# Half sums of g and softmax normalizations in another order on VectorE, in a fused sparse-attention and PReLU-MLP kernel

## The chip, the cores and the metric

The kernel runs on one core of one Trainium2 chip. The metric is device time in microseconds (us). One execution was also recorded by the hardware profiler; all durations of single instructions are from that execution. Engines are named as in the profile: PE is TensorE (matmuls, with PEld for its weight loads), DVE is VectorE, ACT is ScalarE, POOL is GpSimd, SP issues most of the DMAs.

## What is computed

Two things in a row. First, sparse attention for 8 batches, 8 heads, 576 tokens and a head dimension of 64: four heads look at the last 32 tokens, four at every 32nd token. Then a two-layer MLP on the 4608 token rows of width 512, with 2048 hidden values and a PReLU:

```
scores = where(mask, q @ k.T / 8, -1e9);  attn = softmax(scores);  x = attn @ v      # 4608 x 512
h = x @ w_in                                                                          # 4608 x 2048
g = max(h, 0) + alpha * min(h, 0)
out = g @ w_out                                                                       # 4608 x 512
```

## The kernel before, in words

**Chunks.** The MLP runs over nine chunks of 512 rows, n = 0 to 8. Layer 1 of a chunk is sixteen pieces (`lin1_piece`, L596): four matmuls of 128x512 into a PSUM bank (L608), ACT makes relu(-h) (L616), and DVE combines both into a 128x512 block of g in fp16 (L619). The attention of later batches is woven in between: after each piece of the MLP, `attn_n` (L827) runs none, one or two attention steps from a long list (L500 to L570).

**Layer 2 with fewer multiplications.** For chunks 2 to 8 (`FAST = 2`) layer 2 is `lin2_fast` (L696), Strassen's scheme in Winograd's form: seven products of half-size blocks in place of eight. It needs four sums of the blocks of g, `gsum[0]` to `gsum[3]`, as the stationary operand of some of its matmuls. `g_sum(n, z, h, eng)` (L666) makes half h of sum z: one `tensor_tensor` on 128x1024 fp16 values (L677), with both inputs and the output in SBUF. In the text, (z,h) stands for that half sum. (2,0) and (0,0) are made on POOL during layer 1; the other six are made on DVE.

Each of the fourteen steps of `lin2_fast` is eight matmuls of 128x256. Steps 16 and 17 of the chunk's loop need g alone. Step 18 needs half 0 of sum 0, step 19 half 1 of it: (0,1). Step 20 needs (1,0), step 21 needs (1,1). Steps 22 and 23 need g, steps 24 and 25 sum 2, steps 26 and 27 sum 3, steps 28 and 29 g.

**Attention steps.** A pair is two heads of a batch. `score_both` (L356) makes the scores of a pair: matmuls into the bank `sp` and two banks `sph` (L376), exponentials on ACT (L399 and L405), and the mask by multiplication on POOL (L401 and L408). `pv_piece` (L413) multiplies by v into a bank `pv` (L429, six or four small matmuls), then DVE takes the reciprocal of the row sums (L436) and multiplies (L438). These two DVE instructions together are called a normalization here. A pair of the strided heads has three such pieces, and the last of them is followed by the DMA transpose of the pair's result on SP (L468).

**Banks.** `pv`, `sph` and the transposes of q and k share one pool of three PSUM banks, `pspool` (L63), handed out in turn: the fourth tile waits until the first one's reader is through. For `pv` that reader is the second instruction of the normalization.

**Order.** Every engine runs its instructions in the order of the program (`keep_in_program_order`), so a half sum's place on DVE is where the loop of L953 calls `g_sum`: after the piece of the MLP and the attention steps of step i, by the table `sums` (L949). Counting L964 to L967 out gives, with P for a normalization:

| chunk | attention in steps 16 to 22 |
|---|---|
| 2 | 16: transposes of q; 17: P (pair 14, second); 19: transposes of k; 20: P (pair 14, third); 21: scores; 22: P |
| 3, 4, 5 | 16: P (first of pair 18, 22, 26); 17: P (second); 19: P (third); 20: scores; 21: P (first of the next pair) |
| 6 | 16: scores; 17: P (first of pair 30); 19: P (second); 20: P (third); 22: P |
| 7, 8 | none, the attention is over |

Of the kernel before, what the change touches and what calls it, by code (L numbers as in the profile page):

```python
# [32 lines left out]
def kernel(  # L33
# [540 lines left out]
    def attn_until(b):  # L574

        return max(i for i, (g, _) in enumerate(pieces) if g == 4 * b + 3) + 1
# [3 lines left out]
    def attn_step(end):  # L580
        while late:
            late.pop(0)()
        if pos["i"] < end:
            pieces[pos["i"]][1]()
            pos["i"] += 1
        if defer:
            defer.pop(0)()
        while after:
            after.pop(0)()
# [6 lines left out]
    def lin1_piece(n, m, begin=False):  # L596
        if n not in gTs:
            gTs[n] = gpool.tile([128, 16, 512], F16, tag="gT", name="gT")
        c0 = (512 * n) % RING
        hps = begun.pop(m, None)  # L600
        if hps is None:
            pool, tag = (pspool, "ps") if n == 0 and m // 3 % 2 else (phpool, "hps")
            hps = pool.tile([128, 512], F32, tag=tag, name="hps")
            order = (2, 3, 0, 1)
        else:
            order = (0, 1)
        for kk in order[0:2] if begin else order:
            keep(nc.tensor.matmul(  # L608
                hps, win16[:, kk, 128 * m : 128 * m + 128], xT[:, kk, c0 : c0 + 512],
                start=(kk == 2), stop=(kk == 1)))  # L610
        if begin:
            begun[m] = hps
            return

        neg = npool.tile([128, 512], F32, tag="neg", name="neg")
        keep(nc.scalar.activation(neg, hps, AF.Relu, scale=-1.0))  # L616

        def fin():
            keep(nc.vector.scalar_tensor_tensor(  # L619
                gTs[n][:, m, :], neg, oma[:, m : m + 1], hps, op0=ALU.mult, op1=ALU.add))  # L620
        late.append(fin)
# [3 lines left out]
    def lin2_piece(n, i):  # L625
        mt, part = i // 4, i % 4
        last = n == NCH - 1
        if part == 0:
            ops_cur["t"] = phpool.tile([128, 512], F32, tag="hps", name="ops")
        ops = ops_cur["t"]  # L630
        r0 = 512 * n + 128 * mt
        if last and mt == 3:

            if part in (1, 3):
                return
            c0 = 128 * part
            half = phpool.tile([128, 512], F32, tag="hps", name="ops3") if part else ops
            for kf in range(16):
                keep(nc.tensor.matmul(
                    half[:, 0:256], gTs[n][:, kf, 128 * mt : 128 * mt + 128],  # L640
                    wout16[:, kf, c0 : c0 + 256], start=(kf == 0), stop=(kf == 15)))
            osb = opool.tile([128, 512], F32, tag="osb", name="osb")
            keep(nc.vector.tensor_copy(osb[:, 0:256], half[:, 0:256]))
            keep(nc.sync.dma_start(out[r0 : r0 + 128, c0 : c0 + 256], osb[:, 0:256]))
            return
        for kf in range(4 * part, 4 * part + 4):
            keep(nc.tensor.matmul(  # L647
                ops, gTs[n][:, kf, 128 * mt : 128 * mt + 128], wout16[:, kf, :],
                start=(kf == 0), stop=(kf == 15)))
        if part == 3:  # L650
            osb = opool.tile([128, 512], F32, tag="osb", name="osb")
            keep(nc.scalar.copy(osb, ops))
            keep(nc.sync.dma_start(out[r0 : r0 + 128, :], osb))


    def wout_sum(i):

        def w(j, c):
            return wout16.rearrange("p (i j) c -> p i j c", j=2)[:, :, j, 256 * c : 256 * c + 256]

        o, a, b = (
            (0, w(0, 1), w(0, 0)), (1, w(1, 1), wsum[0]),
            (2, w(1, 1), w(0, 1)), (3, w(1, 0), wsum[1]))[i]
        keep(nc.vector.tensor_tensor(wsum[o], a, b, op=ALU.subtract))

    def g_sum(n, i, h, eng="dve"):  # L666

        gv = gTs[n].rearrange("p (i j) c -> p i j c", j=2)
        hs = slice(4 * h, 4 * h + 4)

        def g(t, j):
            return gv[:, hs, j, 256 * t : 256 * t + 256]

        a, b, op = (
            (g(1, 0), g(1, 1), ALU.add), (gsum[0][:, hs], g(0, 0), ALU.subtract),
            (g(0, 0), g(1, 0), ALU.subtract), (g(0, 1), gsum[1][:, hs], ALU.subtract))[i]
        keep((nc.vector if eng == "dve" else nc.gpsimd).tensor_tensor(gsum[i][:, hs], a, b, op=op))  # L677
# [149 lines left out]
    def attn_n(n, end):  # L827
        for _ in range(n):
            attn_step(end)
        if n == 0:  # L830
            attn_step(0)
# [109 lines left out]
    for pr in range(2):  # L941
# [5 lines left out]

    FAST = 2
    sums = {  # L949
        5: [(2, 0, "pool")], 9: [(0, 0, "pool")], 15: [(0, 1, "dve"), (1, 0, "dve")],  # L950
        16: [(1, 1, "dve")], 18: [(2, 1, "dve")], 19: [(3, 0, "dve")], 20: [(3, 1, "dve")]}

    for n in range(1, NCH):  # L953
        ab = attn_until(n + 1) if n + 1 < B else len(pieces)
        left = ab - pos["i"]
        acc = -1.5 if n == 1 else 0.0
        for i in range(32 if n < FAST else 30):
            if i < 16:
                lin1_piece(n, i if n < FAST else 8 * (i // 8) + 2 * (i % 4) + i % 8 // 4)
            elif n < FAST:  # L960
                lin2_piece(n, i - 16)
            else:
                lin2_fast(n, i - 16)
            acc += left / (22 if n < FAST else 19.5 if n == B - 2 else 21) * (0.5 if i < 16 else 1.0)  # L964
            cnt = int(acc)
            acc -= cnt
            attn_n(cnt, ab)  # L967
            if n < FAST:
                if i in (18, 21, 24, 27):
                    wout_sum((i - 18) // 3)  # L970
                continue
            for z, h, eng in sums.get(i, ()):
                g_sum(n, z, h, eng)
        while pos["i"] < ab:
            attn_step(ab)
# [30 lines left out]
```

## Time and profile before

| what | value |
|---|---|
| median of 3 runs | 299.93 us (299.72 to 301.21) |
| the profiled execution | 299.7 us |
| its span, first to last instruction of the program | 297.8 us |
| half sums on DVE | 42, of 0.68 us each where nothing holds them up |
| half sums on POOL | 14, of 2.12 us |
| normalizations' multiplications (L438) | 62, mean 0.53 us |

How to read the views: a timeline has one row for a run of like instructions on one engine, with its start (us from the span's start), its length, the engine and line, the operation, output and inputs, and how many there are (x16). In square brackets stands how long the engine was idle ahead of it and who ended that. A PE row's length includes the pipeline's drain, so the next row can start before the row's end; distances between starts are what counts.

### The profile page before, as it was taken

How to read it: one execution, taken by the hardware profiler on the slowest of the kernel's cores; microseconds unless marked ns; L12 is line 12 of the kernel's file. 1: busy time of each engine (PE TensorE's matmuls, PEld its weight loads, DVE VectorE, ACT ScalarE, POOL GpSimd, SP SyncE). 2: the span in 40 equal slices, each digit the busy share in tenths (PEclk: the TensorE clock that was granted, in tenths of full speed). 3: DMA queues.
4: the chain of work that ended last, by engine and by line, in shares of the span. 5: the costliest groups of instructions: out<-in, count | busy, mean ns of one | idle time of the engine just before them, and what ended most of it. 6: DMA issues, size and time to landing. Idle time of an engine off the chain costs nothing.

```text
span 297.8 us, 6836 instructions
## 1 busy us (share of the span) xinstructions
PE 292.2 (98%) x2684; PEld 183.0 (61%) x2684; DVE 219.3 (74%) x406; ACT 178.4 (60%) x332; POOL 175.1 (59%) x164
## 2 busy tenths in 40 slices
PE   8999999999999999999999999999999999999995
PEld 3764554544554477646864686468745964784484
DVE  5688886768776897588848984898489948926852
ACT  1777756597557774775477647764676356516730
POOL 8471580059869998979896987595563405002300
PEclk9999999999999999999999999999999999999999
DMA  7999999998995969999999999987711140022004
GB/s 189 257 197 201 263 194 265 223 213 267 126 207 121 121 94 108 212 145 132 138 156 171 152 145 161 182 106 78 212 22 21 23 142 2 0 73 70 0 2 142
DMA packets 96976, 41.18 MB, mean 138 GB/s; under 512 B 75360, under 2 KB 93232, under 8 KB 96944
## 3 DMA queue, kind: packets, MB, share of 16 engines
q0 software_dynamic: 51008, 17.77, 58.4%
q1 hardware_dynamic: 45584, 22.32, 35.1%
q10 hardware_dynamic: 352, 0.66, 0.8%
q8 instruction: 21, 0.34, 0.5%
q14 instruction: 11, 0.09, 0.1%
HBM read 38.24 MB, written 9.44 MB: 160 GB/s over the span
## 4 chain that ended last, share of the span: by engine, by line
PE 85%; DVE 7%; ACT 4%; issue 3%; DVEq 0%; ACTq 0%
PE hps L608 38%; PE ops L743 18%; PE ops L647 5%; PE ops L733 5%; PE pv L429 4%; PE ops L908 3%; PE wps L785 3%; DVE gsum L677 2%; PE sp L376 2%; DVE gT L619 2%; DVE x16s L438 2%; PE sph L376 1%; ACT neg L616 1%; PE xp L454 1%; PE ops L923 1%
## 5 line engine op out<-in xcount | busy, mean ns | idle before, releaser
L608 PE MATMUL hps<-xT,win 128*128 128x512 f16 x576 | 132.4, 379 | 0.0
L619 DVE SCALAR_TENSOR_TENSOR gT<-neg,oma,hps 128x512 f16<-128x512 f32 x144 | 105.3, 744 | 36.3 <-ACT neg L616 28.5
L616 ACT ACTIVATE neg<-hps 128x512 f32<-128x512 f32 x144 | 85.8, 598 | 34.4 <-PE hps L608 32.2
L608 PEld LDWEIGHTS <-win 128*128 128x128 f16 x576 | 53.5, 98 | 58.2 <-issue 0.2
L677 POOL TENSOR_TENSOR gsum<-gT 128x1024 f16<-128x1024 f16 x14 | 29.7, 2124 | 41.7 <-DVE gT L619 36.7
L401 POOL TENSOR_TENSOR et<-et,consts 128x576 f16<-128x576 f16 (+1 forms) x24 | 35.5, 1478 | 29.3 <-ACT et L399 29.2
L743 PEld LDWEIGHTS <-gT 128*128 128x128 f16 x336 | 31.5, 98 | 5.4 <-issue 0.3
L438 DVE TENSOR_TENSOR x<-pv,rc 96x384 f16<-96x384 f32 (+2 forms) x62 | 33.0, 532 | 2.1
L408 POOL TENSOR_TENSOR et<-et,consts 128x576 f16<-128x576 f16 (+1 forms) x24 | 31.4, 1309 | 0.0
L429 PEld LDWEIGHTS <-et 72*128 72x128 f16 (+1 forms) x448 | 23.5, 98 | 12.0 <-DVE et L396 1.1
L743 PE MATMUL ops<-wout,gT 128*128 128x256 f16 x224 | 27.9, 272 | 0.1
L733 PE MATMUL ops<-wsum,gsum 128*128 128x256 f16 x216 | 26.6, 273 | 0.0
L399 ACT ACTIVATE et<-sp 128x576 f16<-128x576 f32 (+1 forms) x24 | 15.5, 644 | 17.1 <-PE sp L376 17.1
L234 POOL COPY vs<-stv 72x1024 f16<-72x1024 f16 x14 | 15.3, 1103 | 15.7 <-DMA stv<-in_v_dram 15.7
L743 PEld LDWEIGHTS <-gsum 128*128 128x128 f16 x224 | 20.9, 98 | 2.6
L733 PEld LDWEIGHTS <-gsum 128*128 128x128 f16 x224 | 20.8, 98 | 2.6
L436 DVE RECIPROCAL rc<-pv 72x6 f32<-72x6 f32 (+2 forms) x80 | 14.7, 184 | 9.8 <-PE pv L429 9.5
L688 DVE TENSOR_TENSOR osb<-ops,par 128x512 f32<-128x512 f32 (+1 forms) x14 | 9.4, 673 | 15.7 <-PE ops L743 8.2
L405 ACT ACTIVATE et<-sph 128x288 f16<-128x288 f32 (+1 forms) x48 | 18.8, 409 | 0.0
L686 ACT COPY osb<-ops 128x512 f32<-128x512 f32 x14 | 8.2, 586 | 16.8 <-PE ops L743 16.7
L647 PE MATMUL ops<-wout,gT 128*128 128x512 f16 x64 | 16.4, 379 | 0.0
L429 PE MATMUL pv<-vs,et 72*128 72x65 f16 x256 | 15.4, 193 | 0.8 <-DVE et L396 0.6
(110 smaller groups left out, 356.5 us busy)
## 6 DMA issues: line engine op xcount, KB each, us to landing
out_dram<-osb SPq DMA_DIRECT2D x35, 256.0 KB, 4.3
vl<-in_v_dram POOLq DMA_DIRECT2D x6, 384.0 KB, 9.3
win<-in_moe_w_in_dram POOLq DMA_DIRECT2D x4, 512.0 KB, 16.6
wout<-in_moe_w_out_dram POOLq DMA_DIRECT2D x4, 512.0 KB, 15.6
qsd<-in_q_dram POOLq DMA_DIRECT2D x7, 288.0 KB, 6.7
ksd<-in_k_dram POOLq DMA_DIRECT2D x7, 288.0 KB, 7.2
stv<-in_v_dram POOLq DMA_DIRECT2D x7, 288.0 KB, 7.8
ql<-in_q_dram SPq DMA_DIRECT2D x3, 576.0 KB, 7.1
```

Source lines behind the costliest of these rows:

```text
L401: keep(nc.gpsimd.tensor_tensor(mv, mv, m, op=ALU.mult))
L405: keep(nc.scalar.activation(ev[:, n * y : n * y + n], sps[y][0:r, 0:n], AF.Exp, scale=SCALE))
L408: keep(nc.gpsimd.tensor_tensor(mv, mv, m, op=ALU.mult))
L429: keep(nc.tensor.matmul(pv[:, 65 * x : 65 * x + 65], et[0:r, c : c + 128], v16[0:r, 2 * P.pr + hh, t, :] if P.strided else v16[:, 6 * (2 * ...
L438: keep(nc.vector.tensor_tensor(P.x16[0:w, c0 : c0 + 64 * nb].rearrange("r (c e) -> r c e", e=64), pvv[:, :, 0:64], rc[0:w, 0:nb].unsqueeze ...
L608: keep(nc.tensor.matmul(hps, win16[:, kk, 128 * m : 128 * m + 128], xT[:, kk, c0 : c0 + 512], start=(kk == 2), stop=(kk == 1)))
L616: keep(nc.scalar.activation(neg, hps, AF.Relu, scale=-1.0))
L619: keep(nc.vector.scalar_tensor_tensor(gTs[n][:, m, :], neg, oma[:, m : m + 1], hps, op0=ALU.mult, op1=ALU.add))
L647: keep(nc.tensor.matmul(ops, gTs[n][:, kf, 128 * mt : 128 * mt + 128], wout16[:, kf, :], start=(kf == 0), stop=(kf == 15)))
L677: keep((nc.vector if eng == "dve" else nc.gpsimd).tensor_tensor(gsum[i][:, hs], a, b, op=op))
L733: keep(nc.tensor.matmul(o, gsum[i][:, y, 128 * z : 128 * z + 128], wsum[i][:, y, :], start=(x == "5" and y == 0 and (z == 0 or alone)), st ...
L743: keep(nc.tensor.matmul(o, lhs(y), rhs(y), start=(first and y == 0), stop=(y == 7), skip_group_check=True))
```

## The change

Two tables take the place of one: `sums2` for chunk 2, and a later `sums` for chunks 3 to 8.

```diff
     sums = {
-        5: [(2, 0, "pool")], 9: [(0, 0, "pool")], 15: [(0, 1, "dve"), (1, 0, "dve")],
-        16: [(1, 1, "dve")], 18: [(2, 1, "dve")], 19: [(3, 0, "dve")], 20: [(3, 1, "dve")]}
+        5: [(2, 0, "pool")], 9: [(0, 0, "pool")], 16: [(0, 1, "dve"), (1, 0, "dve")],
+        17: [(1, 1, "dve")], 19: [(2, 1, "dve")], 20: [(3, 0, "dve"), (3, 1, "dve")]}
+    sums2 = {
+        5: [(2, 0, "pool")], 9: [(0, 0, "pool")], 15: [(0, 1, "dve")],
+        17: [(1, 0, "dve"), (1, 1, "dve")], 19: [(2, 1, "dve")], 20: [(3, 0, "dve"), (3, 1, "dve")]}
...
-            for z, h, eng in sums.get(i, ()):
+            for z, h, eng in (sums2 if n == FAST else sums).get(i, ()):
                 g_sum(n, z, h, eng)
```

The sums themselves, their engines, and the two on POOL stay as they are. On DVE the order from step 15 to step 21 becomes, with "g" for the last block of g (L619) and P1, P2, P3 for the three normalizations of the pair in work:

| chunk | before | after |
|---|---|---|
| 2 | g, (0,1), (1,0), (1,1), P2, (2,1), (3,0), P3, (3,1) | g, (0,1), P2, (1,0), (1,1), (2,1), P3, (3,0), (3,1) |
| 3, 4, 5 | g, (0,1), (1,0), P1, (1,1), P2, (2,1), P3, (3,0), (3,1) | g, P1, (0,1), (1,0), P2, (1,1), P3, (2,1), (3,0), (3,1) |
| 6 | g, (0,1), (1,0), (1,1), P1, (2,1), P2, (3,0), P3, (3,1) | g, (0,1), (1,0), P1, (1,1), P2, (2,1), P3, (3,0), (3,1) |
| 7, 8 | g, (0,1), (1,0), (1,1), (2,1), (3,0), (3,1) | the same |

## The prediction

> **What bounds the kernel now.** I read the page's totals first, then the sums of each chunk, the list of waits, and last the timelines of PE, DVE and POOL around steps 16 to 21.
>
> ```profile
> span 297.8 us, 6836 instructions
> PE 292.2 (98%) x2684; PEld 183.0 (61%) x2684; DVE 219.3 (74%) x406; ACT 178.4 (60%) x332; POOL 175.1 (59%) x164
> ```
>
> PE is the bound: nothing else is busy for more than three quarters of the span. The sums by stage give chunk 3, from the first matmul of its layer 1 to that of chunk 4 (columns: us, then PE, PEld, DVE, ACT and POOL busy, each with its count, clock, DMA share, GB/s):
>
> ```profile
> 122.47:152.78 30.31, 30.25 (x298) 20.02 (x296) 23.34 (x44) 18.70 (x35) 27.13 (x25) 1.00 1.33 153
> ```
>
> PE is busy 30.25 of 30.31 us there, at the full clock. A PE row's length holds the drain of its pipeline, so a short pause is hidden in that figure. What the change can win is time in which PE stands still, and the list of waits names two such places that end with a normalization on DVE (columns: us in total, times, longest).
>
> ```profile
> PEld L376 <- DVE x16s L438: 0.6, 3, 0.2
> PEld L429 <- DVE x16s L438: 0.5, 1, 0.5
> ```
>
> Three waits of a score matmul and one of a `pv` matmul, each for the second instruction of a normalization. The three are in chunks 3, 4 and 5, the one in chunk 2. These numbers are idle time of the weight loader, not PE's loss, so I measure the loss on PE's own rows. Chunk 3:
>
> ```profile
> 138.51 0.35 PE L429 MATMUL pv<-vs,et 72*128 72x65 f16 x6
> 139.75 1.91 PE L733 MATMUL ops<-wsum,gsum 128*128 128x256 f16 x16
> 141.50 0.29 PE L429 MATMUL pv<-vs,et 72*128 72x65 f16 x4
> 141.62 1.04 PE L733 MATMUL ops<-wsum,gsum 128*128 128x256 f16 x8
> 142.59 0.30 PE L376 MATMUL sp<-qT,kT 64*128 64x96 f16 x6
> 142.73 0.56 PE L376 MATMUL sph<-qT,kT 64*128 64x96 f16 x6
> 143.22 1.05 PE L733 MATMUL ops<-wsum,gsum 128*128 128x256 f16 x8
> 144.22 0.34 PE L429 MATMUL pv<-vs,et 72*128 72x65 f16 x6
> ```
>
> Undisturbed, sixteen matmuls take 141.50 - 139.75 = 1.75 us from start to start, 0.109 each, so eight take 0.875. The `sph` group of 142.73 takes 0.49 until the next row. In chunk 2 the same group follows without a wait:
>
> ```profile
> 111.14 1.05 PE L733 MATMUL ops<-wsum,gsum 128*128 128x256 f16 x8
> 112.44 0.30 PE L429 MATMUL pv<-vs,et 72*128 72x65 f16 x4 [0.25 <-DVE x16s L438]
> ...
> 113.68 0.29 PE L376 MATMUL sph<-qT,kT 64*128 64x96 f16 x6
> 113.90 1.05 PE L743 MATMUL ops<-wout,gT 128*128 128x256 f16 x8
> ```
>
> There it takes 0.22. So chunk 3 loses 0.49 - 0.22 = 0.27 us at `sph`. The eight matmuls at 143.22 take 1.00 until `pv` at 144.22: 0.125 more than 0.875, a second, smaller loss. In chunk 2, the eight at 111.14 take 1.30 until `pv`: 0.43 lost. Chunk 5 shows the same two losses as chunk 3 (0.49 and 1.00):
>
> ```profile
> 203.36 0.56 PE L376 MATMUL sph<-qT,kT 64*128 64x96 f16 x6
> 203.85 1.05 PE L733 MATMUL ops<-wsum,gsum 128*128 128x256 f16 x8
> 204.85 0.34 PE L429 MATMUL pv<-vs,et 72*128 72x65 f16 x6
> ```
>
> **Why PE waits there.** The three banks of `pspool` go round. In chunk 3 the order is P1, P2, P3, `sph`, `sph`, next `pv`: the second `sph` takes P2's bank, the next `pv` takes P3's. In chunk 2 two transposes of k stand between, and P3's `pv` takes P2's bank. DVE in chunk 3:
>
> ```profile
> 137.60 1.61 DVE L619 SCALAR_TENSOR_TENSOR gT<-neg,oma,hps 128x512 f16<-128x512 f32 x2 [0.47 <-ACT neg L616]
> 139.25 1.10 DVE L677 TENSOR_TENSOR gsum<-gT 128x1024 f16<-128x1024 f16 x1
> 140.27 0.68 DVE L677 TENSOR_TENSOR gsum<-gsum,gT 128x1024 f16<-128x1024 f16 x1
> 140.87 0.18 DVE L436 RECIPROCAL rc<-pv 72x6 f32<-72x6 f32 x1
> 141.09 0.55 DVE L438 TENSOR_TENSOR x16s<-pv,rc 72x384 f16<-72x384 f32 x1
> 141.56 0.68 DVE L677 TENSOR_TENSOR gsum<-gsum,gT 128x1024 f16<-128x1024 f16 x1
> 142.38 0.55 DVE L438 TENSOR_TENSOR x16s<-pv,rc 72x384 f16<-72x384 f32 x1
> 143.66 0.42 DVE L438 TENSOR_TENSOR x16s<-pv,rc 72x256 f16<-72x256 f32 x1
> ```
>
> P2 ends at 142.38 + 0.55 = 142.93, and PE loads the weights of the `sph` matmul that waited 0.06 later:
>
> ```profile
> 142.99 0.15 PEld L376 LDWEIGHTS <-kT 64*128 64x128 f16 x5 [0.20 <-DVE x16s L438]
> ```
>
> P3 ends at 144.08, and `pv` starts at 144.22. DVE works without a pause from 139.25 on, with three half sums ahead of P2 and four ahead of P3.
>
> **The change, part by part.** Nothing is added or removed: six half sums a chunk stay, none issues a DMA, no row of POOL's or SP's program moves. Only DVE's order changes. From the rows above, a sum holds DVE for 140.87 - 140.27 = 0.60 when undisturbed, a normalization of six for 0.22 (140.87 to 141.09) plus 0.47 (141.09 to 141.56) = 0.69; a result is complete 0.08 after the next instruction starts.
>
> *Chunks 3, 4, 5, the gain.* P1 can start as soon as the last g is off, 139.21 - 0.08 = 139.13, as its `pv` (138.51 + 0.35) is done. P1 runs to 139.82, then (0,1) to 140.42, (1,0) to 141.02, P2 until 141.71 with its result at 141.79. The second `sph` is due at 142.73: it no longer waits. Then (1,1) until 142.31, and P3 with its result at 142.31 + 0.22 + 0.42 = 142.95, over 0.8 ahead of the next `pv`, which then comes at about 143.8. Both losses go: 0.27 + 0.125 = 0.395 a chunk, 1.19 in three.
>
> *Chunks 3, 4, 5, the price.* (0,1) moves behind P1, and step 19 waits for it; behind that wait stands the rest of PE's program. Its first matmul is due at 139.75 + 8 x 0.109 = 140.62. By the above, (0,1) starts at 139.82, ends at 139.82 + 0.68 = 140.50, and with 0.06 for the signal PE has it at 140.56: in time by 0.06. That holds if the sum takes 0.68. In the row it takes 1.10, and the next thing to decide is why.
>
> ```profile
> 107.57 1.27 POOL L401 TENSOR_TENSOR et<-et,consts 72x576 f16<-72x576 f16 x1
> 108.81 1.73 POOL L408 TENSOR_TENSOR et<-et,consts 72x576 f16<-72x576 f16 x1
> ...
> 138.51 1.28 POOL L408 TENSOR_TENSOR et<-et,consts 72x576 f16<-72x576 f16 x1
> 139.73 2.98 POOL L116 DMA_DIRECT2D kr<-in_k_dram x4
> ```
>
> ```profile
> 108.28 1.12 DVE L677 TENSOR_TENSOR gsum<-gT 128x1024 f16<-128x1024 f16 x1
> 109.33 2.36 DVE L677 TENSOR_TENSOR gsum<-gsum,gT 128x1024 f16<-128x1024 f16 x2
> 111.83 0.55 DVE L438 TENSOR_TENSOR x16s<-pv,rc 72x384 f16<-72x384 f32 x1
> ...
> 257.70 0.69 DVE L677 TENSOR_TENSOR gsum<-gT 128x1024 f16<-128x1024 f16 x1
> ```
>
> In chunk 3 a mask runs on POOL from 138.51 to 139.79, and the sum's 0.60 of work, counted back from 140.27, begins at 139.67, as the mask ends. In chunk 2 the first sum overlaps a mask that ends at 108.84 and finishes 0.6 after that; the second mask then stretches to 1.73 and the second sum ends about 0.6 after it. In chunk 7, with no masks left, the same first sum takes 0.69. So the long sums are sums that stood behind a mask. In the new order P1, which reads PSUM, fills the time until the mask is off: (0,1) starts at 139.82, 0.15 after 139.67. I take 0.68, the nearest row, and keep 1.10 as the other end: then (0,1) ends at 140.92, and PE waits until 140.98, 0.36 a chunk, 1.1 in three.
>
> The Trainium skill ("SBUF — State Buffer", section "SBUF: two separate sides") says that VectorE and GpSimd share one pair of SBUF ports under a lock that is held for a whole instruction, and that a VectorE operation with two SBUF inputs takes part in this against a GpSimd operation that reads SBUF. The rows above agree with it: first come, first served, and the loser stands still. By it the sum costs 0.68 in its new place; by the row taken as it stands, 1.10.
>
> *Chunk 2.* (0,1) keeps its place and ends at 109.40. P2 follows at 109.33, ends at 110.10, where it ended at 112.38. P3's `pv`, due at 111.14 + 0.875, has its bank: 0.43 gone. (1,0) moves behind P2, but it stood behind the mask until 110.5 anyway, and still ends 0.68 before the pair's end, 109.33 + 2.36 - 0.60 = 111.09, when step 20 starts as before. (1,1) ends at 111.69, due at 112.15.
>
> *Chunk 6* has scores in step 16, so the first two sums keep their place, and its `pv` banks were never late. *Chunks 7 and 8* have the same order as before. All zero. *What is late next:* (2,1) follows P3 in chunk 3 and ends at about 143.6; step 24, which reads it, lies sixteen matmuls (1.75) behind the `pv` of 143.8, at 145.7 or later. (3,0) and (3,1) end 1.2 after (2,1), and step 26 is sixteen matmuls further. The DMA transpose on SP follows P3 and starts earlier.
>
> The sum: 0.43 + 1.19 = 1.6 at most, less up to 0.05 a chunk for a sum that is just in time: **1.5 us**. Between these places PE is busy without a pause, and the other engines follow it, so what PE wins stays. Against the profiled execution: 299.7 - 1.5 = 298.2. The median lies 0.2 above that execution, so 298.4.
>
> **The rivals.**
>
> *The sum stays long (1.10) wherever it stands.* Then PE waits 0.36 in step 19 of three chunks: gain 1.5 - 1.1 = 0.4, 299.5. For it: it is the first sum behind g in all rows of 1.10. Against it: chunk 7's 0.69.
>
> *The waits were not worth their length*: PE, early by 1.5 us, waits somewhere else for ACT, DVE or a load, and the time stays at about 299.9. For it: DVE is 74% busy. Against it: no other wait of this kind stands in the list, and ACT, POOL and DVE take their pace from PE in each chunk.
>
> *Slower.* (0,1) meets a mask that starts ahead of it. It now starts 0.57 later, so a POOL operation that begins between 139.25 and 139.82 gets in front, and the sum waits for it, 1.27 as in the row of 107.57. PE would stand from 140.62 until 141.83, 1.2 a chunk, 3.6 in three, against 1.5 won: 302.0. It decides from the point where POOL's mask begins 0.7 later than in the row of 138.51. Against it: the mask of 138.51 is the last before four DMA issues at 139.73, and POOL's place is set by ACT and so by PE. The Trainium skill's rule of the lock ("SBUF — State Buffer", section "SBUF: two separate sides") would let this happen; no row shows it behind P1.
>
> *More than forecast.* All of the 1.6 comes, and the runs fall, like the lowest of those before, 0.2 below the median from which I count: 298.1 or less.
>
> **How the numbers follow.** Forecast 0.60, long sum 0.14, no gain 0.11, slower 0.06, more than forecast 0.09. A measurement of this kernel tells about 0.5% from no change, 1.50 us: faster means below 298.43. The forecast's own range, 298.0 to 298.9, straddles that, so I split it: 0.31 below, 0.29 above. Faster 0.31 + 0.09 = 0.40; same 0.29 + 0.14 + 0.11 = 0.54; slower 0.06. The range reaches from 297.9 to 300.1: it holds the forecast, the long sum and no gain, and leaves out the slower case and part of the last.
>
> **What would show it.** Right: no wait of L376 or L429 for x16s in chunks 2 to 5; the `sph` group 0.22 from start to next row; (0,1) after P1, 0.68 long, and sixteen matmuls of steps 18 and 19 in 1.75; chunk 3 at 29.9 us. Wrong: a gap in the middle of these sixteen, a sum of 1.1 behind P1, or the same 0.4 us lost elsewhere in the chunk.

## The result and the profile after

| | median | lowest to highest | runs |
|---|---|---|---|
| before | 299.87 us | 298.85 to 301.21 | 12 |
| changed | 298.35 us | 297.80 to 299.17 | 12 |

The ratio is 0.9952, with a 95% interval of 0.9937 to 0.9967: 1.45 us faster (1.0 to 1.9). The forecast was 298.4. That it lies 0.05 from the median is luck: the interval is 0.9 us wide.

The profiled execution of the changed kernel spans 296.8 us, 1.0 less than the one of before. The rest is hidden by its start: it reaches chunk 2 0.48 later, ahead of anything that the change touches. The clean measure is PE's first matmul of each chunk. First the rows before:

```profile
90.85 2.32 PE L608 MATMUL hps<-xT,win 128*128 128x512 f16 x10
...
122.31 1.89 PE L608 MATMUL hps<-xT,win 128*128 128x512 f16 x8
...
213.24 1.03 PE L608 MATMUL hps<-xT,win 128*128 128x512 f16 x4
```

The first row is chunk 2's, the second chunk 3's, the third chunk 6's. The same three in the changed kernel:

```profile
91.33 1.89 PE L608 MATMUL hps<-xT,win 128*128 128x512 f16 x8
...
122.38 0.81 PE L608 MATMUL hps<-xT,win 128*128 128x512 f16 x3
...
212.19 1.24 PE L608 MATMUL hps<-xT,win 128*128 128x512 f16 x5
```

Chunk 2 goes from 31.46 to 31.05 us, 0.41 less. Chunks 3 to 5 go from 90.93 to 89.81, 1.12 less, 0.37 each. From there to the end it is 84.6 in both. Together 1.53.

In the list of waits no weight load waits for `x16s` any more. (`x16s` is where the normalizations P1, P2 and P3 write: 18 multiplications. The 62 of the table ahead of the prediction are those that write `x`.) In chunk 2 of the changed kernel `pv` of step 20 comes 0.88 after the eight matmuls ahead of it, where it came 1.30 after:

```profile
111.64 1.05 PE L733 MATMUL ops<-wsum,gsum 128*128 128x256 f16 x8
112.52 0.29 PE L429 MATMUL pv<-vs,et 72*128 72x65 f16 x4
```

PE in chunk 3 of the changed kernel:

```profile
138.59 0.35 PE L429 MATMUL pv<-vs,et 72*128 72x65 f16 x6
...
139.83 1.91 PE L733 MATMUL ops<-wsum,gsum 128*128 128x256 f16 x16
141.58 0.29 PE L429 MATMUL pv<-vs,et 72*128 72x65 f16 x4
141.71 1.04 PE L733 MATMUL ops<-wsum,gsum 128*128 128x256 f16 x8
142.68 0.30 PE L376 MATMUL sp<-qT,kT 64*128 64x96 f16 x6
142.81 0.29 PE L376 MATMUL sph<-qT,kT 64*128 64x96 f16 x6
143.04 1.05 PE L733 MATMUL ops<-wsum,gsum 128*128 128x256 f16 x8
143.92 0.35 PE L429 MATMUL pv<-vs,et 72*128 72x65 f16 x6
```

The `sph` group takes 0.23 from its start to the next row where it took 0.49, the eight matmuls behind it 0.88 where they took 1.00, and the sixteen of steps 18 and 19 still take 1.75. DVE and POOL in the same place:

```profile
139.43 0.55 DVE L438 TENSOR_TENSOR x16s<-pv,rc 72x384 f16<-72x384 f32 x1
139.91 0.68 DVE L677 TENSOR_TENSOR gsum<-gT 128x1024 f16<-128x1024 f16 x1
140.50 0.68 DVE L677 TENSOR_TENSOR gsum<-gsum,gT 128x1024 f16<-128x1024 f16 x1
...
141.32 0.55 DVE L438 TENSOR_TENSOR x16s<-pv,rc 72x384 f16<-72x384 f32 x1
```

```profile
138.58 1.28 POOL L408 TENSOR_TENSOR et<-et,consts 72x576 f16<-72x576 f16 x1
```

(0,1) takes 0.68, not 1.10: the mask on POOL ends at 139.86, under P1. It is complete at 140.59, and PE's first matmul that reads it is due at 139.83 + 8 x 0.109 = 140.70. With the 0.06 for the signal it is in time by 0.05. P2 is complete at 141.87, almost a microsecond ahead of `sph`.

### The profile page after: what moved, and what is told of

Its sections match the earlier page's. It is cut to its first block, busy times and chain, and to the rows that moved or that the text cites. A ratio compares the mean times of both kernels' runs of the same rounds, so it can differ in the third digit from the quotient of the medians.

```text
span 296.8 us, 6835 instructions
## 1 busy us (share of the span) xinstructions
PE 290.4 (98%) x2684; PEld 182.7 (62%) x2684; DVE 216.6 (73%) x406; ACT 178.8 (60%) x332; POOL 173.6 (58%) x164
## 4 chain that ended last, share of the span: by engine, by line
PE 92%; DVE 2%; DMA 2%; ACT 2%; issue 0%; SPq 0%; DVEq 0%; ACTq 0%
PE hps L608 41%; PE ops L743 21%; PE ops L733 8%; PE ops L647 5%; PE pv L429 4%; PE ops L908 2%; PE sp L376 2%; DMA consts<-consts 2%; PE xp L454 1%; PE ops L923 1%; PE tp L292 1%; PE sph L376 1%; PE tf L154 1%; DVE x L438 1%; ACT qT L230 1%; DVE gT L619 1%
## 5 line engine op out<-in xcount | busy, mean ns | idle before, releaser
L619 DVE SCALAR_TENSOR_TENSOR gT<-neg,oma,hps 128x512 f16<-128x512 f32 x144 | 105.3, 744 | 36.3 <-ACT neg L616 28.5
L401 POOL TENSOR_TENSOR et<-et,consts 128x576 f16<-128x576 f16 (+1 forms) x24 | 33.8, 1409 | 27.5 <-ACT et L399 27.2
L408 POOL TENSOR_TENSOR et<-et,consts 128x576 f16<-128x576 f16 (+1 forms) x24 | 31.4, 1309 | 0.0
L234 POOL COPY vs<-stv 72x1024 f16<-72x1024 f16 x14 | 15.3, 1104 | 17.5 <-DMA stv<-in_v_dram 17.5
```

Of the source, the lines that this page charges most:

```text
L401: keep(nc.gpsimd.tensor_tensor(mv, mv, m, op=ALU.mult))
L408: keep(nc.gpsimd.tensor_tensor(mv, mv, m, op=ALU.mult))
L619: keep(nc.vector.scalar_tensor_tensor(gTs[n][:, m, :], neg, oma[:, m : m + 1], hps, op0=ALU.mult, op1=ALU.add))
```

## The experiments

The kernels of the experiments are called e1 to e11. In each trace the length of a chunk is taken as above, from PE's first matmul of the chunk to that of the next; a table of them stands at the end of this section.

**Is it the sum of independent parts? (e1, e2)** The changed kernel, in e1 with the new order in chunk 2 alone, in e2 in the later chunks alone.

```diff
 # e1: the table of chunks 3 to 8, back to that of before
     sums = {
-        5: [(2, 0, "pool")], 9: [(0, 0, "pool")], 16: [(0, 1, "dve"), (1, 0, "dve")],
-        17: [(1, 1, "dve")], 19: [(2, 1, "dve")], 20: [(3, 0, "dve"), (3, 1, "dve")]}
+        5: [(2, 0, "pool")], 9: [(0, 0, "pool")], 15: [(0, 1, "dve"), (1, 0, "dve")],
+        16: [(1, 1, "dve")], 18: [(2, 1, "dve")], 19: [(3, 0, "dve")], 20: [(3, 1, "dve")]}
 # e2: the table of chunk 2, back to that of before
     sums2 = {
-        5: [(2, 0, "pool")], 9: [(0, 0, "pool")], 15: [(0, 1, "dve")],
-        17: [(1, 0, "dve"), (1, 1, "dve")], 19: [(2, 1, "dve")], 20: [(3, 0, "dve"), (3, 1, "dve")]}
+        5: [(2, 0, "pool")], 9: [(0, 0, "pool")], 15: [(0, 1, "dve"), (1, 0, "dve")],
+        16: [(1, 1, "dve")], 18: [(2, 1, "dve")], 19: [(3, 0, "dve")], 20: [(3, 1, "dve")]}
```

> The new order in chunk 2 alone; chunks 3 to 8 as before. Theory (PE loses what it waits for late normalizations, chunk by chunk): the 0.43 us before pv of step 20 in chunk 2 goes, the losses of chunks 3 to 5 (0.49 at sph, 1.00 for the eight matmuls behind it) stay: 0.4 us faster than before, ratio about 0.9985. Rival (the gain comes from elsewhere, or one part alone carries it): no change, or all of 1.5.

> The new order in chunks 3 to 8, chunk 2 as before. Theory: three times 0.395 us, 1.2 faster than before, ratio about 0.996; chunk 2 keeps its 0.43 (1.30 from the eight matmuls to pv). Rival (the parts are not independent, PE loses part of it again later): under 0.8.

Measured: e1 0.9980 (0.9968 to 0.9992), 0.6 us faster; e2 0.9949 (0.9933 to 0.9964), 1.5 faster. Both expected values lie in the intervals. The ratios alone don't show that the parts add up: e2's interval holds the 0.9952 of the whole change too, and 0.6 and 1.5 are more than 1.45 together. The traces show it. In e1 chunk 2 lasts 31.15 and chunks 3 to 5 last 30.30 to 30.32, as before; in e2 chunk 2 lasts 31.47, as before, and chunks 3 to 5 last 29.93, as in the changed kernel. Each kernel keeps just the other part's waits. First e1, then e2:

```profile
PEld L376 <- DVE x16s L438: 0.6, 3, 0.2
```

```profile
PEld L429 <- DVE x16s L438: 0.5, 1, 0.5
```

**Does the order matter, or only when the normalizations end? (e8)** The kernel before, with one sum less on DVE ahead of P2: the half sum (1,1) of chunks 3 to 5 is left out.

```diff
             for z, h, eng in sums.get(i, ()):
-                g_sum(n, z, h, eng)
+                if n not in (3, 4, 5) or (z, h) != (1, 1):
+                    g_sum(n, z, h, eng)
```

> The kernel before, with the half sum (1,1) of chunks 3 to 5 left out, so that its PE matmuls read the one of an earlier chunk. The order is that of before; DVE is only 0.60 less late. Theory (what counts is when the normalizations end): P2 ends at about 142.3 and P3 at 143.5 on the clock of before, both ahead of their due times, and the losses of 0.27 and 0.125 go: 1.2 faster than before, ratio 0.996. Rival (the losses belong to the place of the sph group and the pv behind it, not to DVE): no change.

Measured: 0.9972 (0.9957 to 0.9987), 0.8 us faster; 1.2 is in the interval. PE in chunk 3:

```profile
142.62 0.29 PE L376 MATMUL sph<-qT,kT 64*128 64x96 f16 x6
142.84 1.05 PE L733 MATMUL ops<-wsum,gsum 128*128 128x256 f16 x8
143.73 0.35 PE L429 MATMUL pv<-vs,et 72*128 72x65 f16 x6
```

0.22 and 0.89, with the sums in the old order, and chunks 3 to 5 last 29.93, as in the changed kernel: both losses are DVE's lateness and nothing that belongs to these matmuls.

**Can the sums go further back? (e3)** As the changed kernel, with (0,1) and (1,0) of chunks 3 to 5 behind P2.

```diff
+    sums3 = {
+        5: [(2, 0, "pool")], 9: [(0, 0, "pool")], 17: [(0, 1, "dve"), (1, 0, "dve")],
+        18: [(1, 1, "dve")], 19: [(2, 1, "dve")], 20: [(3, 0, "dve"), (3, 1, "dve")]}
...
-            for z, h, eng in (sums2 if n == FAST else sums).get(i, ()):
+            for z, h, eng in (sums2 if n == FAST else sums3 if n in (3, 4, 5) else sums).get(i, ()):
```

> As the changed kernel, but in chunks 3 to 5 (0,1) and (1,0) stand behind the second normalization too. Theory (a half sum has a due time, which (0,1) meets by 0.06 us in the changed kernel): (0,1) comes 0.69 later, PE stands 0.6 in the middle of the sixteen matmuls of steps 18 and 19, three times: 1.9 slower than the changed kernel, 0.4 slower than before, ratio about 1.0013. Rival (the sums have slack, so the normalizations alone matter): as the changed kernel, 0.995.

Measured: 1.0023 (1.0007 to 1.0040), slower than before, and 2.1 us slower than the changed kernel by the two ratios.

```profile
139.36 1.04 PE L733 MATMUL ops<-wsum,gsum 128*128 128x256 f16 x8
140.99 1.05 PE L733 MATMUL ops<-wsum,gsum 128*128 128x256 f16 x8 [0.60 <-DVE gsum L677]
```

Step 19 starts 1.63 after step 18 in place of 0.87: 0.76 lost, in each of three chunks. (0,1) is complete 1.57 after the start of step 18, where it was 0.76 after it in the changed kernel: 0.81 later, not the 0.69 expected, as P2 now waits a little for its own `pv`. 0.81 later costs 0.76, so the place that the change chose has 0.05 of slack, as computed above.

**Why was the first sum long? (e7)** The kernel before, with the mask that ran under that sum left out.

```diff
-                if y:
+                if y and P.g not in (19, 23, 27):
                     keep(nc.gpsimd.tensor_tensor(mv, mv, m, op=ALU.mult))
```

> The kernel before, with the last mask ahead of layer 2 in chunks 3 to 5 left out (half of those scores stay unmasked). Theory (the first sum behind g takes 1.10 because it stands behind that mask): (0,1) takes 0.68 in its old place, DVE is 0.42 earlier, P2 and P3 are ready ahead of their due times, and 0.395 goes three times: 1.2 faster than before, ratio 0.996, with the sums in the old order. Rival (the first sum behind g is always long): 1.10 as before, no change.

Measured: 0.9970 (0.9954 to 0.9986), 0.9 us faster; 1.2 is in the interval.

```profile
139.16 0.69 DVE L677 TENSOR_TENSOR gsum<-gT 128x1024 f16<-128x1024 f16 x1
```

(0,1) takes 0.69 in its old place, so its 1.10 was the mask's doing. Both losses of chunks 3 to 5 are gone in this trace too: these chunks last 29.93. But two chunks that the edit doesn't touch lost more than before, chunk 2 0.84 (31.46 to 32.30) and chunk 6 0.51 (29.04 to 29.55). Chunk 2 is taken up below.

**Does POOL shut the sums out, and who wins? (e4, e5, e6, e9)** A second, dependent application of the same mask, in the changed kernel and in the one before; then a memset in its place; then a memset ahead of the mask.

```diff
 # e4 (changed kernel) and e5 (kernel before); pairs 19, 23 and 27 are those of chunks 3 to 5
                 if y:
                     keep(nc.gpsimd.tensor_tensor(mv, mv, m, op=ALU.mult))
+                    if P.g in (19, 23, 27):
+                        keep(nc.gpsimd.tensor_tensor(mv, mv, m, op=ALU.mult))
 # e6 (changed kernel), in the same place; scratch is a tile of its own, 128x1536
+                    if P.g in (19, 23, 27):
+                        keep(nc.gpsimd.memset(scratch, 0.0))
 # e9 (changed kernel), ahead of that mask; scratch is 128x1100
+                if y and P.g in (19, 23, 27):
+                    keep(nc.gpsimd.memset(scratch, 0.0))
                 if y:
```

> The kernel before with the same second mask. Theory: (0,1) still starts as the first mask ends, the second mask waits for it and then holds up (1,0) and all of DVE behind it by 1.18, so the second sph matmul comes 1.18 later in each of three chunks: 3.5 slower than before, ratio about 1.012. Rival (no lock): no change.

> The changed kernel, with the last mask ahead of layer 2 in chunks 3 to 5 applied twice on POOL (the mask is 0 or 1). Theory (a DVE sum with two SBUF inputs and a POOL operation that reads SBUF shut each other out, first come first served): the second mask runs from 139.8 to 141.1, starts 0.1 ahead of (0,1), which then ends about 1.15 later; PE stands 1.0 in each of three chunks: 3.0 slower than the changed kernel, 1.5 slower than before, ratio about 1.005. Rival (no such lock; the first sum behind g was long for another reason): as the changed kernel, 0.995.

Measured: e5 1.0116 (1.0094 to 1.0138), 3.5 us slower, as expected in sum. In its trace chunks 3 to 5 are 1.11 longer each, where 1.18 was expected, and chunk 2 is 0.85 longer, see below. The second mask waits for (0,1) and then holds up (1,0), which takes 1.76 in place of 0.68:

```profile
140.62 1.61 POOL L410 TENSOR_TENSOR et<-et,consts 72x576 f16<-72x576 f16 x1
```

```profile
141.03 1.76 DVE L679 TENSOR_TENSOR gsum<-gsum,gT 128x1024 f16<-128x1024 f16 x1
```

e4 0.9949 (0.9936 to 0.9963), where 1.005 was expected: a miss. The DVE and POOL rows of e4 say why (the lines of code have moved by two):

```profile
139.36 0.68 DVE L679 TENSOR_TENSOR gsum<-gT 128x1024 f16<-128x1024 f16 x1
139.96 0.68 DVE L679 TENSOR_TENSOR gsum<-gsum,gT 128x1024 f16<-128x1024 f16 x1
...
141.25 1.07 DVE L679 TENSOR_TENSOR gsum<-gsum,gT 128x1024 f16<-128x1024 f16 x1
```

```profile
139.42 2.36 POOL L410 TENSOR_TENSOR et<-et,consts 72x576 f16<-72x576 f16 x1
```

The second mask depends on the first and starts at 139.42, 0.06 behind (0,1) and not 0.1 ahead of it. It takes 2.36 in place of 1.28, as it stands through (0,1) and (1,0); then it holds up (1,1), which had time. So the two do shut each other out, but the timing of who is first was wrong by 0.16. Two more kernels ask the same with nothing that the mask depends on (e9) and with a POOL operation that reads no SBUF (e6):

> The changed kernel, with a memset of 128x1100 fp16 on POOL (about 1.0 us, by 1.38 for 128x1536) ahead of the last mask before layer 2 in chunks 3 to 5. The mask then starts at about 139.6 on the changed kernel's clock, 0.3 ahead of (0,1), without waiting for anything else. Theory (whoever starts first holds the other off; the second mask of the earlier run lost because the sum started 0.06 ahead of it): the mask keeps its 1.28, (0,1) waits to 140.8 and is 1.5 long, PE stands 0.8 in the middle of the sixteen matmuls, three times: 2.4 slower than the changed kernel, 0.9 slower than before, ratio about 1.003. Rival (the sum always wins): as the changed kernel, 0.995.

> The changed kernel, with a memset of a scratch tile (128x1536 fp16) on POOL in the place of that second mask: it writes SBUF and reads none. Theory, by the Trainium skill (SBUF — State Buffer, section SBUF: two separate sides), under which a DVE operation with two SBUF inputs is shut out only by a GpSimd operation that reads SBUF: no sum is held up, time as the changed kernel, ratio 0.995. Rival (any POOL operation on SBUF shuts the sum out): (0,1) is long by the memset's length, up to 3.0 slower than the changed kernel in sum.

Measured: e9 1.0047 (1.0028 to 1.0065), 1.4 us slower than before, 2.9 slower than the changed kernel by the ratios. e6 0.9953 (0.9934 to 0.9973), as the changed kernel. In e9 the mask starts 0.35 ahead of (0,1), and the sum takes 1.48:

```profile
139.62 1.48 DVE L680 TENSOR_TENSOR gsum<-gT 128x1024 f16<-128x1024 f16 x1
```

```profile
139.27 1.27 POOL L411 TENSOR_TENSOR et<-et,consts 72x576 f16<-72x576 f16 x1
```

PE loses 0.73 in each of three chunks:

```profile
139.56 1.04 PE L736 MATMUL ops<-wsum,gsum 128*128 128x256 f16 x8
141.16 1.05 PE L736 MATMUL ops<-wsum,gsum 128*128 128x256 f16 x8 [0.56 <-DVE gsum L680]
```

Chunk 2 of e9 is 0.45 longer than in the changed kernel as well, see below. That whoever starts first goes first, as the expectation of e9 has it, is more than the traces show. In the kernel before, a mask of chunk 3 starts 0.28 ahead of (3,0), with P3 in work on DVE, and still waits through (3,0) and (3,1), which take 1.28 together as where nothing holds them up:

```profile
143.72 2.69 POOL L401 TENSOR_TENSOR et<-et,consts 128x576 f16<-128x576 f16 x1 [1.01 <-ACT et L399]
```

```profile
144.00 1.28 DVE L677 TENSOR_TENSOR gsum<-gT,gsum 128x1024 f16<-128x1024 f16 x2
```

So 0.35 ahead was enough in e9 and 0.28 was not here. In e6 the memset runs under two sums, and neither is longer for it:

```profile
139.07 0.68 DVE L680 TENSOR_TENSOR gsum<-gT 128x1024 f16<-128x1024 f16 x1
139.67 0.68 DVE L680 TENSOR_TENSOR gsum<-gsum,gT 128x1024 f16<-128x1024 f16 x1
```

```profile
138.97 1.38 POOL L411 MEMSET scratch<- 128x1536 f16 x1
```

This agrees with the Trainium skill ("SBUF — State Buffer", section "SBUF: two separate sides"), by which only a GpSimd operation that reads SBUF shuts out a VectorE operation with two SBUF inputs.

**What happened in chunk 2. (e10, e11)** In e5 and e7, chunk 2's code is that of before, yet its step 20 to `pv` took far longer than the 1.30 us of the trace of before. In e7, POOL, DVE and PE:

```profile
107.63 1.74 POOL L401 TENSOR_TENSOR et<-et,consts 72x576 f16<-72x576 f16 x1
109.33 1.71 POOL L408 TENSOR_TENSOR et<-et,consts 72x576 f16<-72x576 f16 x1
```

```profile
108.17 3.43 DVE L677 TENSOR_TENSOR gsum<-gsum,gT 128x1024 f16<-128x1024 f16 x2
```

```profile
110.12 1.04 PE L733 MATMUL ops<-wsum,gsum 128*128 128x256 f16 x8
112.35 0.30 PE L429 MATMUL pv<-vs,et 72*128 72x65 f16 x4 [1.19 <-DVE x16s L438]
```

The pair (1,0), (1,1) takes 3.43 in place of 2.36, and `pv` comes 2.23 after the eight matmuls' start: 1.36 lost in place of 0.43. POOL reached its two masks later against DVE in that execution, the first 0.27 behind the start of (0,1) where it was 0.71 ahead, and both got in, one ahead of each sum.

Where POOL lost this time stands one chunk earlier. There DVE makes differences of the blocks of w_out (`wsum`, L664, two SBUF inputs), and in e7 three of POOL's masks each waited for one of them:

```profile
75.71 2.27 POOL L408 TENSOR_TENSOR et<-et,consts 72x576 f16<-72x576 f16 x1
79.44 2.59 POOL L401 TENSOR_TENSOR et<-et,consts 72x576 f16<-72x576 f16 x1
82.00 2.24 POOL L408 TENSOR_TENSOR et<-et,consts 72x576 f16<-72x576 f16 x1
```

```profile
79.69 1.21 DVE L664 TENSOR_TENSOR wsum<-wout,wsum 128x2048 f16<-128x2048 f16 x1
```

In the trace of before the same masks take 1.28, 1.30 and 1.28, and POOL then has 3.56 us to spare ahead of its next mask, at 84.15. In e7 nothing is left of that. From this mask on POOL works without a pause in both traces, 23.42 us up to the mask of chunk 2, so what it lost stays. The same three masks are long in e5 and e9, and only in these: in the eight other traces without an edit in chunk 2, none or two of them are. These three are also the traces in which POOL's copy of v (L234), which waits for a DMA load, comes latest: it starts 26.7 to 26.9 us ahead of chunk 2's first matmul, in the other eight 27.5 to 31.0. That the load sets it off fits, but no run tests it. In e9, whose chunk 2 has the new order, the chunk lasts 31.50 in place of 31.05. Between e7 and e9 the new order in chunk 2 is worth 0.80, twice what it is where POOL is not late.

To bring this about at will, a memset of 128x1000 on a tile of its own was put on POOL ahead of the first of the two masks, in both kernels:

```diff
+                if P.g == 15:
+                    keep(nc.gpsimd.memset(scratch, 0.0))
                 keep(nc.gpsimd.tensor_tensor(mv, mv, m, op=ALU.mult))
```

> The kernel before, with a memset of 128x1000 fp16 (about 0.9 us) on POOL ahead of the first of the two masks that meet layer 2 of chunk 2, so that POOL is as late against DVE as it was by itself in two of the earlier runs. Theory: (0,1) loses less, but both masks get in, one between (0,1) and (1,0), one between (1,0) and (1,1); the pair takes 3.4 in place of 2.4, and the wait before pv of step 20 grows from 0.43 to 1.4: 0.95 slower than before, ratio about 1.003. Rival (chunk 2 in those two runs was late for another reason): no change.

> The changed kernel with the same memset. Theory: one mask runs under P2, so that only one holds up the sums; P2 is on time, and (1,1) comes 0.5 late for step 21: 0.5 slower than the changed kernel, ratio about 0.997 to before. Against the kernel before with that memset the new order is then worth about 2.0 in place of 1.5. Rival (the lock costs the same in either order): 0.95 slower than the changed kernel.

Measured: e10 1.0023 (1.0000 to 1.0046), 0.7 us slower than before; e11 0.9971 (0.9955 to 0.9987), 0.6 slower than the changed kernel by the ratios. The expected values lie in the intervals, but so does the rival of e11, 0.95 slower; the traces decide. In e10 the pair takes 3.44, and `pv` waits:

```profile
110.97 1.04 PE L736 MATMUL ops<-wsum,gsum 128*128 128x256 f16 x8
113.02 0.30 PE L432 MATMUL pv<-vs,et 72*128 72x65 f16 x4 [1.01 <-DVE x16s L441]
```

In e11 `pv` is on time, 0.88 after the eight matmuls, and step 21 waits a little for (1,1):

```profile
111.29 1.04 PE L736 MATMUL ops<-wsum,gsum 128*128 128x256 f16 x8
112.17 0.29 PE L432 MATMUL pv<-vs,et 72*128 72x65 f16 x4
112.64 1.05 PE L736 MATMUL ops<-wsum,gsum 128*128 128x256 f16 x8 [0.19 <-DVE gsum L680]
```

1.18 lost in one order, 0.35 in the other. As step 20 itself starts on time in both, where it was about 0.1 late, chunk 2 as a whole is 0.65 longer in e10 (32.11) and 0.24 in e11 (31.29); the expectations had 0.95 and 0.5, without that 0.1. Between the two kernels with the late POOL lie 1.4 us by the medians (300.28 and 298.92), where 2.0 was expected; the intervals allow both, and the chunks of the two traces give 1.96.

**All traces side by side.** Lengths in us; chunks 3, 4 and 5 agree within 0.02 in each trace, so one column stands for them.

| kernel | order in chunk 2 | chunk 2 | order in chunks 3 to 5 | each of chunks 3 to 5 |
|---|---|---|---|---|
| before | old | 31.46 | old | 30.31 |
| changed | new | 31.05 | new | 29.94 |
| e1, new order in chunk 2 alone | new | 31.15 | old | 30.31 |
| e2, new order in chunks 3 to 8 alone | old | 31.47 | new | 29.93 |
| e3, sums behind P2 | new | 31.19 | (0,1) and (1,0) further back | 30.70 |
| e4, mask twice | new | 31.16 | new | 29.93 |
| e5, mask twice | old | 32.31 | old | 31.42 |
| e6, memset behind the mask | new | 31.04 | new | 29.93 |
| e7, mask left out | old | 32.30 | old | 29.93 |
| e8, one sum left out | old | 31.52 | old | 29.93 |
| e9, mask later | new | 31.50 | new | 30.67 |
| e10, POOL late in chunk 2 | old | 32.11 | old | 30.31 |
| e11, POOL late in chunk 2 | new | 31.29 | new | 29.93 |

## Why the prediction was right

- **Where PE stands still.** Four waits for a normalization, read off PE's rows: 0.43 in chunk 2, 0.27 and 0.125 in each of chunks 3 to 5. All are gone; the chunks are shorter by 0.41 and 0.37, against 0.43 and 0.395. e8 shows that in chunks 3 to 5 lateness of DVE is the whole cause: with one sum less they are as short as in the changed kernel. In chunk 2 the wait grows and shrinks with DVE's lateness (e10, e11). The chunks of e1 and e2 show that the parts don't depend on each other. The deduction of up to 0.05 a chunk, for a sum just in time, is not seen: the sixteen matmuls of steps 18 and 19 take 1.75, as undisturbed.
- **The price of moving (0,1).** It was said to be in time by 0.06; counted the same way, with the signal, it is by 0.05. e3 and e9 show that this narrow place is real: 0.81 and 0.78 later, it costs 0.76 and 0.73 a chunk, 0.05 less each.
- **0.68 or 1.10.** The choice rested on the masks' rows; e7 and e9 confirm it from both sides, and the rival of the long sum falls.
- **Chunk 2's (1,0)**, said to stand behind the mask in either order: step 20 starts about 0.1 late in both traces (0.2 in e1, e3 and e4).
- **Chunks 6 to 8**: 84.6 us in both, as said.
- **What is late next**: nothing. The rival in which PE waits elsewhere falls with the 1.53 that arrive.
- **The slower rival** is a true mechanism (e9) whose point is not reached here. The point itself was put too early: "first come, first served" does not hold for the times at which the rows start. A mask was said to get in front as soon as it starts ahead of (0,1); the row of 143.72 shows one that starts 0.28 ahead of a sum and loses, the rows of e9 one that starts 0.35 ahead and wins. The forecast didn't hang on it.

What the prediction did not see: chunk 2's loss ahead of `pv` has a second size, 1.36 in e5 and e7, when POOL is late. Of five traces with the old order in chunk 2 and no edit there (before, e2, e8, e5, e7), two show it, and their chunk 2 is 0.84 and 0.85 longer. Of six with the new order and no edit there (the changed kernel, e1, e3, e4, e6, e9) one meets the late POOL, and its chunk 2 is 0.45 longer. How often it happens in the runs without a profile stays open, and so does its share of the measured 1.45, since the rows of the traces of before and after give 1.53 without it.

## What to carry to other kernels

When PE is the bound, read its rows from start to start: a busy share of 98% hid 1.5 us of waiting. An engine that serves several consumers in program order should serve them in the order of their due times, and each move must be checked against the due time of what is moved back; here the room was 0.05 us. Where two engines lock each other out, an operation that is outside the lock can fill the time: here a normalization, which reads PSUM, took its 0.55 while a mask on POOL took its 1.28.

## What the runs showed of the hardware

- DVE sums with two SBUF inputs and POOL masks exclude each other for the whole of an operation: 0.68 becomes 1.10 (before) or 1.48 (e9), and 1.28 becomes 2.36 (e4). A POOL memset of 1.38 us excluded nothing (e6).
- Which one goes next is not simply the one that starts first. With DVE outside the lock, a mask that started 0.35 ahead of a sum went first (e9) and one that started 0.28 ahead did not (before, 143.72). In e10 a waiting mask, 0.45 ahead of (1,0), got in between two sums that stood back to back; in e4 a mask that started 0.54 ahead of (1,0) waited through two of them. What decides this was not found.
- POOL was 0.98 late at one operation, with no change of the code there, after three masks had waited for DVE 25 us earlier. That moved a loss of PE from 0.43 to 1.36 (e7).
